# Attention times V with V as the stationary operand: four heads in 32-column tiles, output as head dimension by token

## The chip, the cores and the metric

The kernel runs on one core of a Trainium2 chip. The metric is the device time of one execution in microseconds (us), measured several times. Where a ratio of two kernels is given, it is the mean time of the fast runs of one over that of the fast runs of the kernel before in the same rounds, so it is not quite the ratio of the medians that are quoted beside it.

The engines are named as the profile names them: PE is TensorE (matmul), PEld its weight loads, DVE is VectorE, ACT is ScalarE, POOL is GpSimd, SP only issues DMAs.

## The reference

One transformer-like block over 2048 tokens of width 576: windowed attention with 32 heads of 18 elements, gated by a feed-forward network.

```python
def _A_ref(x, wqkv, wo):                      # x: layernormed, (1, 2048, 576)
    H = 32; Dh = 18; W = 256
    q, k, v = ...                             # x @ wqkv, split in heads
    scores = einsum("bhqd,bhkd->bhqk", q, k) * Dh ** -0.5
    mask = (0 <= i - j) & (i - j < W)
    p = softmax(where(mask, scores, -1e9))
    o = einsum("bhqk,bhkd->bhqd", p, v)
    return o.transpose(0, 2, 1, 3).reshape(B, S, D) @ wo
def _B_ref(x, w_gate, w_up, w_down):          # F = 4608
    return (sigmoid(x @ w_gate) * (x @ w_up)) @ w_down
out = x + _A_ref(xn, ...) * silu(_B_ref(xn, ...))
```

## The kernel before

The program is written as a graph of operations, each with an engine, an estimated duration and dependencies. A list scheduler in the kernel's own Python puts them in a fixed order on each engine, using the estimates; on the chip each engine then runs its list in order and waits on semaphores. Work goes in four blocks of 512 tokens. Attention goes by groups of four heads (8 groups per block, 32 in all), and the feed-forward matmuls (gate/up, then down) of the block stand between its pieces.

PSUM is cut into two pools of two units (a unit is two banks): pool S for attention, projections and transposes, pool F for the feed-forward network.

```python
self.pool_s = Pool("S", [0, 1])
self.pool_f = Pool("F", [2, 3])
```

A score visit computes up to four 128x128 blocks for four heads and takes **both** units of pool S:

```python
h = self.pool_s.hold(2)
...            # matmuls with 32-row tiles, then exp on ACT, mask multiply on DVE
```

The product with V (PV) uses the exponentials as the stationary operand, so the output has tokens on partitions. The last column of V is ones, which gives the softmax sum beside each output. Three small VectorE operations normalise; the unit of PSUM is free after the first of them.

```python
hp = self.pool_s.hold()
def f_pv(eng):                                 # 96 matmuls with 19 columns per group (72 in the first block)
    for i in range(BPC):
        for h4 in range(4):
            for n, kb in enumerate(kbs):
                res = pair(eng, [b[:, o:o + 19] for b in outs],
                           lambda r, t: self.expr[r, se, h4, at * P:(at + 1) * P],
                           lambda r, t: self.v_aug[r, kb % NVB, hg * 4 + h4, :], ...)
sm = op("DVE", dve_ns(608), f_sum, ...)        # adds the two row halves, PSUM -> SBUF
hp.release(sm)
rc = op("DVE", 120, lambda e: e.reciprocal(self.rrec[:, sr, :], out[:, :, DH]), ...)   # 128x16
on = op("DVE", dve_ns(288), f_on, ...)         # o_tok = pvs * rrec
```

After the eight groups, each 128 tokens are transposed on PE (18 small matmuls), copied out of PSUM by VectorE and multiplied with wo.

The softmax here doesn't subtract the row's maximum and nothing guards it: scores larger than these inputs give would overflow.

## Time and profile before

The median is 602.46 us (three runs, 599.55 to 611.99, the last of them slow). The profiled execution took 602.5 us, of which 600.8 us are in the trace.

| | before |
|---|---|
| span of the trace | 600.8 us |
| PE / DVE / ACT / POOL busy | 98% / 55% / 50% / 26% |
| chain of waits that ended last | 94% PE |
| mean granted PE clock | 0.992 |

The busy line of the page, and below it the waits view for PE (engine and line, what it waited for, us in total, number of times, longest):

```profile
PE 587.5 (98%) x10424; PEld 345.8 (58%) x10424; DVE 329.5 (55%) x631; ACT 297.8 (50%) x397; POOL 156.9 (26%) x316
```

```profile
PE ps L62 <- DMA wgs<-in_B_w_up_dram: 3.5, 2, 2.4
PE ps L434 <- DVE xnr L405: 1.7, 2, 0.9
...
```

PE is the limit, and it waits for almost nothing: about 8 us in all. What PV costs is read from the timeline of PE (start us, length us, engine, line, operation, tiles, count). One head group, in the second block:

```profile
214.68 1.36 PE L62 MATMUL ps<-v_aug,expr 64*128 64x19 bf16 x96
215.89 2.10 PE L62 MATMUL ps<-xnT,wgs 64*128 64x512 bf16 x18
217.93 0.40 PE L565 MATMUL ps<-qT,kT 18*128 18x256 bf16 x12
218.26 2.98 PE L62 MATMUL ps<-xnT,wgs 64*128 64x512 bf16 x26
```

Lengths overlap by the depth of the pipeline, so starts are what to subtract: PV holds PE from 214.68 to 215.89, which is 1.21 us; a score visit holds it for 0.33 us. The VectorE part of the same work, from the groups of instructions (busy us, mean ns of one, idle before):

```profile
L620 DVE TENSOR_REDUCE pvs<-ps 128x304 f32<-128x608 f32 x32 | 25.3, 791 | 16.2 <-PE ps L62 16.2
L632 DVE TENSOR_TENSOR o_tok<-pvs,rrec 128x288 bf16<-128x288 f32 x32 | 14.6, 458 | 1.1
L625 DVE RECIPROCAL rrec<-pvs 128x16 f32<-128x16 f32 x32 | 8.1, 254 | 1.1
```

### The profile page before, as it was taken

The page shows a single profiled execution, that of the slowest core. Times are in us where ns is not written, and L with a number is a line of the kernel's source. Part 1 is how long each engine was busy: PE and PEld are TensorE (multiplying, and loading weights), DVE is VectorE, ACT ScalarE, POOL GpSimd, SP SyncE. Part 2 cuts the span into 40 slices and gives each one's busy share as a digit, 9 for nine tenths or more (in the row PEclk, how much of TensorE's full clock was granted, in tenths as well). Part 3 has the DMA queues.
Part 4 walks back from the last instruction along what each step waited for, and adds up shares of the span by engine and source line. Part 5 has one row for each costly group of instructions (what it writes and reads, how often), then busy time and mean ns, then how long its engine had stood idle before and what let it go on. Part 6 is the DMA issues. An engine that isn't in the chain of part 4 may idle for free.

```text
span 600.8 us, 22967 instructions
## 1 busy us (share of the span) xinstructions
PE 587.5 (98%) x10424; PEld 345.8 (58%) x10424; DVE 329.5 (55%) x631; ACT 297.8 (50%) x397; POOL 156.9 (26%) x316
## 2 busy tenths in 40 slices
PE   6999999999999999999999999999999999999996
PEld 5554544577764444567775454446777545445775
DVE  4336576626567676554546666565444766556122
ACT  3135456455275666564265666564245565675111
POOL 3190410710554105200554005200555016000000
PEclk8999999999999999999999999999999999999999
DMA  9999999900044754540202565553020364650010
GB/s 192 191 199 214 212 208 220 175 8 23 24 119 118 184 131 113 135 102 2 61 20 60 138 142 129 134 123 82 21 58 25 96 143 105 158 122 4 2 42 21
DMA packets 112050, 63.89 MB, mean 106 GB/s; under 512 B 12208, under 2 KB 109936, under 8 KB 111952
## 3 DMA queue, kind: packets, MB, share of 16 engines
q1 hardware_dynamic: 101552, 57.08, 43.8%
q0 software_dynamic: 9216, 4.75, 3.4%
q8 instruction: 82, 1.34, 1.0%
q10 hardware_dynamic: 1184, 0.59, 0.5%
q14 instruction: 16, 0.13, 0.1%
HBM read 55.30 MB, written 2.36 MB: 96 GB/s over the span
## 4 chain that ended last, share of the span: by engine, by line
PE 94%; DMA 3%; DVE 1%; ACT 1%; issue 0%; SPq 0%; ACTq 0%; DVEq 0%
PE ps L62 87%; PE ps L565 5%; DMA wgs<-in_B_w_up_dram 3%; PE ps L434 1%; ACT expr L581 0%; SPq L206 0%; DVE pvs L620 0%; ACT L362 0%; DVE o_tok L632 0%; DVE s_attn L817 0%; DVE thf L822 0%; ACTq L206 0%; DVE hT L735 0%; ACT tring L732 0%; DVE rrec L625 0%
## 5 line engine op out<-in xcount | busy, mean ns | idle before, releaser
L62 PE MATMUL ps<-xnT,wgs 64*128 64x512 bf16 (+1 forms) x2628 | 300.3, 377 | 4.2 <-DMA wgs<-in_B_w_up_dram 3.5
L581 ACT ACTIVATE expr<-ps 128x1024 bf16<-128x1024 f32 (+1 forms) x192 | 179.5, 969 | 69.2 <-PE ps L565 69.2
L62 PEld LDWEIGHTS ps<-xnT,wgs 64*128 64x128 bf16 x2628 | 122.3, 95 | 144.4 <-issue 9.1
L62 PE MATMUL ps<-wd_sb,hT 64*128 64x288 bf16 x2304 | 151.9, 283 | 0.0
L589 DVE TENSOR_TENSOR expr<-expr,mask 128x768 bf16<-128x768 bf16 (+2 forms) x192 | 93.9, 491 | 103.4 <-ACT expr L581 103.2
L732 ACT ACTIVATE tring<-ps 128x512 bf16<-128x512 f32 x144 | 86.0, 597 | 124.4 <-PE ps L62 124.4
L206 POOL DMA_DIRECT2D qT<-qd x144 | 73.4, 509 | 280.0 <-DVE qd L471 156.5
L735 DVE SCALAR_TENSOR_TENSOR hT<-tring,ps 128x512 bf16<-128x512 bf16 x144 | 99.1, 688 | 58.8 <-ACT tring L732 56.2
L62 PEld LDWEIGHTS ps<-wd_sb,hT 64*128 64x128 bf16 x2304 | 108.3, 94 | 30.9 <-issue 3.5
L206 POOL DMA_DIRECT2D kT<-qd x144 | 73.3, 509 | 0.0
L62 PEld LDWEIGHTS ps<-v_aug,expr 64*128 64x128 bf16 x2880 | 41.0, 93 | 7.1 <-issue 1.2
L62 PE MATMUL ps<-v_aug,expr 64*128 64x19 bf16 x2880 | 41.3, 168 | 0.6 <-issue 0.6
L62 PE MATMUL ps<-xnT,wqk 64*128 64x512 bf16 (+1 forms) x360 | 38.1, 355 | 0.5 <-ACT expr L581 0.5
L565 PE MATMUL ps<-qT,kT 18*128 18x256 bf16 (+1 forms) x960 | 37.0, 245 | 0.0
L565 PEld LDWEIGHTS ps<-qT,kT 18*128 18x128 bf16 x960 | 15.7, 92 | 35.6 <-issue 21.9
L471 DVE CAST qd<-ps 128x1024 bf16<-128x1024 f32 (+1 forms) x20 | 22.3, 1117 | 24.9 <-PE ps L62 24.9
L620 DVE TENSOR_REDUCE pvs<-ps 128x304 f32<-128x608 f32 x32 | 25.3, 791 | 16.2 <-PE ps L62 16.2
L807 ACT ACTIVATE thf<-ps 128x576 bf16<-128x576 f32 (+1 forms) x20 | 11.1, 555 | 46.4 <-PE ps L62 45.9
L398 POOL TENSOR_TENSOR rstd<-veps,neghalf 128x1 f32<-128x1 f32 x16 | 9.0, 570 | 72.7 <-DVE veps L396 72.6
L673 ACT ACTIVATE s_attn<-ps 128x576 bf16<-128x576 f32 x16 | 10.4, 650 | 34.9 <-PE ps L62 34.9
L62 PEld LDWEIGHTS ps<-xnT,wqk 64*128 64x128 bf16 x360 | 17.2, 94 | 17.1 <-ACT expr L581 1.9
L420 ACT ACTIVATE xnT<-ps 128x1152 bf16<-128x1152 bf16 x15 | 16.4, 1130 | 8.5 <-PE ps L434 8.4
(45 smaller groups left out, 215.8 us busy)
## 6 DMA issues: line engine op xcount, KB each, us to landing
wgs<-in_B_w_gate_dram SPq DMA_DIRECT2D x71, 288.0 KB, 4.0
wgs<-in_B_w_up_dram SPq DMA_DIRECT2D x71, 288.0 KB, 4.8
wd_sb<-in_B_w_down_dram SPq DMA_DIRECT2D x9, 576.0 KB, 9.9
xf<-in_A_x_dram SPq DMA_DIRECT2D x16, 144.0 KB, 3.4
out_dram<-xf SPq DMA_DIRECT2D x16, 144.0 KB, 1.9
qT<-qd POOLq DMA_DIRECT2D x112, 18.0 KB, 2.0
kT<-qd POOLq DMA_DIRECT2D x112, 18.0 KB, 2.0
xr<-in_A_x_dram SPq DMA_DIRECT2D x6, 288.0 KB, 4.5
```

The costliest lines, as they stand in the source:

```text
L62: res = eng.matmul(outs[i], lhs(ROWS[t], i), rhs(ROWS[t], i), start=start, stop=stop, tile_position=(64 * t, 0))
L206: o = self.op(eng, DMA_ISSUE_NS[eng], lambda e: e.dma_start(dst, src), name, deps, prio, nbytes=nbytes)
L420: return eng.activation(dst, self.tr_src(h), ACTF.Copy)
L471: return eng.tensor_copy(dst, self.both(h, n))
L565: res = eng.matmul(self.ps[:, o:o + nq * P], self.kT[r, kp, ko:ko + P], self.qT[r, qs, q0 * P:(q0 + nq) * P], start=True, stop=True, tile_ ...
L581: return eng.activation(self.expr[:, se, 2 * u:2 * u + 2, 0:n], src, ACTF.Exp, scale=SM_SCALE)
L589: return eng.tensor_tensor(e_, e_, m_, ALU.mult)
L620: return eng.tensor_reduce(self.pvs[:, pt, :], self.both(hp, 304).rearrange("p t q -> p q t"), mybir.AxisListType.X, ALU.add)
L673: return eng.activation(dst, self.both(h2, 288), ACTF.Copy, scale=0.25)
L732: th = op("ACT", act_ns(NT), lambda e: e.activation(self.tring[:, st, :], bank(h, 0), ACTF.Tanh, scale=0.5), f"th:{c}:{ft}", deps=[pg, dt_ ...
L735: mu = op("DVE", dve_ns(NT), lambda e: e.scalar_tensor_tensor(self.hT[:, ft, :], self.tring[:, st, :], 1.0, bank(h, 1), ALU.add, ALU.mult) ...
L807: return e.activation(v2(t)[:, a:b, :], y2()[:, a:b, :], ACTF.Tanh, scale=0.25)
```

## The change

The intent is to take work off PE. V becomes the stationary operand: 19 columns, one 32-column tile per head, so that four heads run side by side, and the tokens stream. The output has the head dimension on partitions (32 per head) and the token along the free axis, which is what wo wants, so the transposes go. A shuffle spreads each head's sum over its 32 partitions, a reciprocal and a multiply normalise, and small DMAs pack the heads from 32-partition to 18-partition spacing. Bundled with it is a new start of the program: more warm-up matmuls used as fillers, three early gate/up tiles instead of two, and the first weights loaded from another queue. The scheduler's estimate for issuing a DMA on the GpSimd queue also goes from 1000 to 600 ns.

```diff
 hp = self.pool_s.hold()
 def f_pv(eng):
-    ... pair(eng, outs, expr (stationary), v_aug (19 moving columns)) ...
+    b = hp.units[0] * 1024
+    for n, (kb, q0, nq, se, at) in enumerate(blocks):
+        for h4 in range(4):
+            res = eng.matmul(self.ps[32 * h4:32 * h4 + DH + 1, b + q0 * P:b + (q0 + nq) * P],
+                             self.v_aug[:, kb % NVB, hg * 4 + h4, :], self.expr[:, se, h4, at * P:(at + nq) * P],
+                             start=(n == 0), stop=(n == len(blocks) - 1), tile_position=(0, 32 * h4), ...)
-sm = op("DVE", dve_ns(608), f_sum, ...)
-hp.release(sm)
-rc = op("DVE", 120, lambda e: e.reciprocal(self.rrec[:, sr, :], out[:, :, DH]), ...)
-on = op("DVE", dve_ns(288), f_on, ...)
+sh = op("DVE", 740, lambda e: e.stream_shuffle(self.den[:, :], pv_out(), [DH] * 32), ..., deps=[pv])
+rc = op("DVE", dve_ns(NT), lambda e: e.reciprocal(self.den[:, :], self.den[:, :]), ..., deps=[sh])
+on = op("DVE", dve_ns(NT), lambda e: e.tensor_tensor(self.onr[:, so, :], pv_out(), self.den[:, :], ALU.mult), ...)
+hp.release(on)
+... 160 DMAs on the GpSimd queue pack onr into oT ...
 def build_wo(self, c):
-    ... 16 x (18 transposes on PE, copy on DVE) ...
 # start of the program
-NWARM = 70
+NWARM = 110
-early = 2 if c == 0 else 0
+early = 3 if c == 0 else 0
 ... (cut)
```

`dve_ns(512)` is 673 ns. The unit of PSUM is now held until the last of the three VectorE operations, because the multiply reads PSUM.

More of the change, by code (lines that the diff above doesn't have):

```diff
@@ L37 @@
 NFIN = 2
-NWARM = 70
+NON = 2
+KT = 5
+COL = 1032
+NWARM = 110
 NQK = 5
-DMA_ISSUE_NS = {"SP": 600.0, "POOL": 1000.0, "ACT": 650.0}
+DMA_ISSUE_NS = {"SP": 600.0, "POOL": 600.0, "ACT": 650.0}
 DMA_LAT_NS = 2500.0
@@ L119 @@
     __slots__ = ("eng", "est", "deps", "fn", "name", "prio", "start", "end", "tok", "needs_tok",
-                 "nbytes", "slack", "idx", "succs", "cidx", "odeps", "acq", "lane", "mode")
+                 "nbytes", "slack", "idx", "succs", "cidx", "odeps", "acq", "lane", "mode", "filler")
     def __init__(self, eng, est, fn, name, deps, prio, nbytes, odeps, acq):
@@ L152, in __init__ @@
         self.slack = 0.0
+        self.filler = None
         for d in self.odeps:
@@ L238, in alloc_memory @@
         assert size([P, BPC, D], bf16) <= size([P, NEX, 4, NT], bf16)
-        self.o_tok, _ = seq("o_tok", [P, BPC, XW])
-        self.oT, _ = seq("oT", [P, 2, KS, P])
+        self.oT, _ = seq("oT", [P, KT, NT])
+        self.onr, _ = seq("onr", [P, NON, NT])
+        self.den, _ = seq("den", [P, NT], f32)
         self.s_attn, _ = seq("s_attn", [P, BPC, D])
@@ L243, in alloc_memory @@
         self.wv_sb, _ = seq("wv_sb", [P, KS, D // 2])
-        self.wo_sb, _ = seq("wo_sb", [P, KS, D // 2])
+        self.wo_sb, _ = seq("wo_sb", [P, KT, D])
         self.qd, _ = seq("qd", [P, NQD, 2, NT])
@@ L256, in alloc_memory @@
         self.rstd, _ = seq("rstd", [P, NST, 1], f32)
-        self.pvs, _ = seq("pvs", [P, 1, 4 * BPC * (DH + 1)], f32)
-        self.rrec, _ = seq("rrec", [P, 2, 4 * BPC], f32)
         if self.verbose:
@@ L272, in build_graph @@
         self.r_ex = Ring(NEX, "expr")
-        self.r_rec = Ring(2, "rrec")
-        self.r_pvs = Ring(1, "pvs")
-        self.r_oT = Ring(2, "oT")
+        self.r_on = Ring(NON, "onr")
         self.r_w = Ring(NWS, "wgs")
@@ L289, in build_graph @@
         self.op_q2 = {}
-        self.otr_last = []
+        self.wo_last = []
+        self.op_oT = []
         self.prev_f2_last = None
@@ L364, in build_consts @@
         h = self.pool_f.hold()
+        w = None
         for i in range(NWARM):
@@ L367, in f_warm @@
                 return pair(eng, self.halves(h, P), lambda r, t: zero[r, :], lambda r, t: zero[r, :], True, True)
-            w = op("PE", 110, f_warm, f"warm:{i}", deps=[z], prio=1, acq=None if i else h, odeps=[w] if i else [])
-        h.release(w)
-        self.ffn_last = w
+            w = op("PE", 110 if i < 36 else 64, f_warm, f"warm:{i}", deps=[z], prio=4, acq=None if i else h, odeps=[w])
+            w.filler = h
+            h.release(w)
         wq, wk, wv = (self.wqkv[:, i * D:(i + 1) * D] for i in range(3))
@@ L413, in f_tr @@
                 return self.transposes(eng, h, lambda r, o: self.xnr[r, sn, o:o + P])
-            tr = op("PE", KS * 29.5, f_tr, f"tr:{st}", deps=[dup, self.op_ident, war], prio=pr, acq=h)
+            tr = op("PE", KS * 29.5, f_tr, f"tr:{st}", deps=[dup, self.op_ident, war], prio=pr if c else 0, acq=h)
             self.r_xn.release(sn, tr)
@@ L551, in build_attn @@
             masks = [(0, 1, 2), (1, 3, 1), (0, 3, 1)]
-        where = {}
+        blocks = []
         ready = []
@@ L573, in build_attn @@
             se, de = self.r_ex.produce()
-            for at_, (kb, q0, nq, at) in enumerate(specs):
-                for i in range(nq):
-                    where[(kb, q0 + i)] = (se, at + i)
+            blocks += [(kb, q0, nq, se, at) for kb, q0, nq, at in specs]
             for u in range(2):
@@ L599, in f_pv @@
             res = None
-            outs = self.halves(hp, 304)
-            for i in range(BPC):
-                kbs = [kb for kb in (k0 + i - 2, k0 + i - 1, k0 + i) if kb >= 0]
+            b = hp.units[0] * 1024
+            for n, (kb, q0, nq, se, at) in enumerate(blocks):
                 for h4 in range(4):
-                    o = i * 76 + h4 * 19
-                    for n, kb in enumerate(kbs):
-                        se, at = where[(kb, i)]
-                        res = pair(eng, [b[:, o:o + 19] for b in outs],
-                                   lambda r, t: self.expr[r, se, h4, at * P:(at + 1) * P],
-                                   lambda r, t: self.v_aug[r, kb % NVB, hg * 4 + h4, :], n == 0, n == len(kbs) - 1)
-            return res
-        pv = op("PE", (48 if c else 36) * 24.7, f_pv, f"pv:{c}:{hg}", deps=[[m for m, _ in ready], vdeps], prio=1, acq=hp)
+                    res = eng.matmul(self.ps[32 * h4:32 * h4 + DH + 1, b + q0 * P:b + (q0 + nq) * P],
+                                     self.v_aug[:, kb % NVB, hg * 4 + h4, :], self.expr[:, se, h4, at * P:(at + nq) * P],
+                                     start=(n == 0), stop=(n == len(blocks) - 1), tile_position=(0, 32 * h4),
+                                     skip_group_check=True)
+            return res
+        pv = op("PE", 30 + sum(57 * b[2] for b in blocks), f_pv, f"pv:{c}:{hg}", deps=[[m for m, _ in ready], vdeps], prio=1, acq=hp)
+        pv.mode = COL
         self.op_pv[(c, hg)] = pv
@@ L614, in build_attn @@
             self.r_ex.release(se, pv)
-        sr, dr = self.r_rec.produce()
-        pt, dp = self.r_pvs.produce()
-        def f_sum(eng):
-            return eng.tensor_reduce(self.pvs[:, pt, :], self.both(hp, 304).rearrange("p t q -> p q t"),
-                                     mybir.AxisListType.X, ALU.add)
-        sm = op("DVE", dve_ns(608), f_sum, f"ps:{c}:{hg}", deps=[pv, dp], prio=1)
-        hp.release(sm)
-        out = self.pvs[:, pt, :].rearrange("p (q d) -> p q d", d=DH + 1)
-        rc = op("DVE", 120, lambda e: e.reciprocal(self.rrec[:, sr, :], out[:, :, DH]), f"rc:{c}:{hg}",
-                deps=[sm, dr], prio=1)
@@ L628, in f_on @@
-        def f_on(eng):
-            src = out[:, :, 0:DH].rearrange("p (q h) d -> p q h d", q=BPC)
-            dst = self.o_tok[:, :, hg * 72:(hg + 1) * 72].rearrange("p q (h d) -> p q h d", d=DH)
-            rr = self.rrec[:, sr, :].rearrange("p (q h) -> p q h", q=BPC)[:, :, :, None].broadcast_to([P, BPC, 4, DH])
-            return eng.tensor_tensor(dst, src, rr, ALU.mult)
-        on = op("DVE", dve_ns(288), f_on, f"on:{c}:{hg}", deps=[rc, self.otr_last], prio=1)
-        self.r_rec.release(sr, on)
@@ L635, in build_attn, with pv_out @@
-        self.r_pvs.release(pt, on)
-        self.op_on[(c, hg)] = on
+        so, do = self.r_on.produce()
+        def pv_out():
+            b = hp.units[0] * 1024
+            return self.ps[:, b:b + NT]
+        sh = op("DVE", 740, lambda e: e.stream_shuffle(self.den[:, :], pv_out(), [DH] * 32), f"den:{c}:{hg}", deps=[pv], prio=1)
+        rc = op("DVE", dve_ns(NT), lambda e: e.reciprocal(self.den[:, :], self.den[:, :]), f"rc:{c}:{hg}", deps=[sh], prio=1)
+        on = op("DVE", dve_ns(NT), lambda e: e.tensor_tensor(self.onr[:, so, :], pv_out(), self.den[:, :], ALU.mult),
+                f"on:{c}:{hg}", deps=[rc, do], prio=1)
@@ new lines, in build_attn @@
+        hp.release(on)
+        for u in range(4 * hg, 4 * hg + 4):
+            d0, end = DH * u, DH * u + DH
+            while d0 < end:
+                d1 = min(end, (d0 // P + 1) * P)
+                p0 = 32 * (u % 4) + d0 - DH * u
+                for r0 in ((d0 % P,) if d0 < 4 * P else (d0 % P, 64 + d0 % P)):
+                    o = self.dma(self.oT[r0:r0 + d1 - d0, d0 // P, :], self.onr[p0:p0 + d1 - d0, so, :], (d1 - d0) * NT * 2,
+                                 f"dma:o:{c}:{u}", ("o", hg), deps=[on, self.wo_last], prio=1, eng="POOL")
+                    self.r_on.release(so, o)
+                    self.op_oT.append(o)
+                d0 = d1
@@ L637, in build_attn @@
         if (c, hg) == (0, 0):
-            self.op_wo_w = self.load_rows(self.wo_sb, self.wo[:, 0:288], self.wo[:, 288:D], "dma:wo", ("wo",), 8, [pv])
+            self.op_wo_w = [self.dma(self.wo_sb[:, 0:4, :], self.wo[0:512, :].rearrange("(k p) c -> p k c", p=P), 512 * D * 2,
+                                     "dma:wo", ("wo", 0), deps=[pv], prio=8)]
+            self.op_wo_w += [self.dma(self.wo_sb[r, 4, :], self.wo[512:D, :], 64 * D * 2, "dma:wo4", ("wo", 1), deps=[pv],
+                                      prio=8) for r in ROWS]
@@ L640, in build_wo @@
     def build_wo(self, c):
         op = self.op
-        last = []
-        dup = op("DVE", 280, lambda e: e.tensor_copy(self.o_tok[:, :, D:XW], self.o_tok[:, :, 0:64]), f"odup:{c}",
-                 deps=[self.op_on[(c, 0)], self.otr_last], prio=1)
-        for i in range(BPC):
-            qb = c * BPC + i
-            h = self.pool_s.hold()
-            so, do = self.r_oT.produce()
-            def f_tr(eng, i=i, h=h):
-                return self.transposes(eng, h, lambda r, o: self.o_tok[r, i, o:o + P])
-            tr = op("PE", KS * 29.5, f_tr, f"otr:{qb}", deps=[[self.op_on[(c, hg)] for hg in range(NHG)], dup, self.op_ident],
-                    prio=1, acq=h)
-            last.append(tr)
-            def f_te(eng, h=h, so=so):
-                dst = self.oT[:, so, :, :].rearrange("p k (t c) -> p t k c", t=2)
-                return eng.tensor_copy(dst, self.tr_src(h))
-            te = op("DVE", dve_ns(KS * P, 1.9), f_te, f"ote:{qb}", deps=[tr, do], prio=1)
-            h.release(te)
-            h2 = self.pool_s.hold()
-            ss = i
-            war = [self.op_q2[qb - BPC]] if c else []
-            def f_wo(eng, h2=h2, so=so):
-                return self.row_proj(eng, h2, lambda r, kt: self.oT[r, so, kt, :], self.wo_sb)
-            wo = op("PE", 9 * mm_ns(288), f_wo, f"wo:{qb}", deps=[te, self.op_wo_w, war], prio=1, acq=h2)
-            self.r_oT.release(so, wo)
-            def f_se(eng, ss=ss, h2=h2):
-                dst = self.s_attn[:, ss, :].rearrange("p (t c) -> p t c", t=2)
-                return eng.activation(dst, self.both(h2, 288), ACTF.Copy, scale=0.25)
-            se = op("ACT", act_ns(D), f_se, f"sev:{qb}", deps=[wo], prio=1)
-            h2.release(se)
-            self.op_s[qb] = se
@@ L677, in build_wo, with wo, f @@
-        self.otr_last = last
+        oT, self.op_oT, self.wo_last = self.op_oT, [], []
+        def wo(i, h, swap, deps, acq):
+            cols = slice(i * P, (i + 1) * P)
+            ks = range(KT - swap)
+            def f(eng):
+                res = None
+                for k in ks:
+                    res = pair(eng, self.halves(h, 288), lambda r, t: self.oT[r, k, cols],
+                               lambda r, t: self.wo_sb[r, k, 288 * t:288 * t + 288], swap == 0 and k == 0,
+                               swap == 1 and k == KT - 2, swap)
+                return res
+            return op("PE", len(ks) * mm_ns(288), f, f"wo:{c * BPC + i}:{swap}", deps=[oT, self.op_wo_w, deps], prio=1, acq=acq)
@@ new lines, in build_wo, with f_se @@
+        for i in range(0, BPC, 2):
+            hs = [self.pool_s.hold() for _ in range(2)]
+            lo = [wo(i + j, hs[j], 0, [self.op_q2[c * BPC + i + j - BPC]] if c else [], hs[j]) for j in range(2)]
+            for j in range(2):
+                qb = c * BPC + i + j
+                hi = wo(i + j, hs[j], 1, [lo[j]], None)
+                self.wo_last.append(hi)
+                def f_se(eng, i=i, j=j, h=hs[j]):
+                    dst = self.s_attn[:, i + j, :].rearrange("p (t c) -> p t c", t=2)
+                    return eng.activation(dst, self.both(h, 288), ACTF.Copy, scale=0.25)
+                se = op("ACT", act_ns(D), f_se, f"sev:{qb}", deps=[hi], prio=1)
+                hs[j].release(se)
+                self.op_s[qb] = se
@@ L687, in build_ffn, with pe @@
             self.op_wd = []
-        def pe(est, fn, name, deps, acq=None):
-            o = op("PE", est, fn, name, deps=deps, prio=3, odeps=[self.ffn_last], acq=acq)
+        def pe(est, fn, name, deps, acq=None, prio=3):
+            o = op("PE", est, fn, name, deps=deps, prio=prio, odeps=[self.ffn_last], acq=acq)
             self.ffn_last = o
@@ L695, in weights @@
             sw, dw = self.r_w.produce()
-            pr = wg if c == 0 and wg < 4 else 3
+            pr = 1 + wg if c == 0 and wg < 4 else 3
             fc = slice(wg * WG * P, (wg + 1) * WG * P)
-            ds = self.load_rows(self.wgs[:, sw, :, :], self.wg[:, fc], self.wu[:, fc], f"dma:w:{c}:{wg}", ("w", sw), pr,
-                                [dw, self.op_tab if c == 0 and wg == 0 else None],
-                                eng="ACT" if c == 0 and wg == 0 else "SP")
+            ds = self.load_rows(self.wgs[:, sw, :, :], self.wg[:, fc], self.wu[:, fc], f"dma:w:{c}:{wg}", ("w", sw), pr, [dw])
             slots[wg] = sw
@@ L727, in f @@
                 return res
-            return pe(len(ks) * mm_ns(n), f, f"f1{half}:{c}:{ft}", [xin, wops[ft // WG]], acq)
+            return pe(len(ks) * mm_ns(n), f, f"f1{half}:{c}:{ft}", [xin, wops[ft // WG]], acq,
+                      3 if part is None else 1)
         def tail(ft, h, pg):
@@ L740, in tail @@
             hm[ft] = mu
-        early = 2 if c == 0 else 0
+        early = 3 if c == 0 else 0
         if early:
             weights(0)
-            hs = [self.pool_f.hold() for _ in range(early)]
+            weights(1)
+            hs = [self.pool_f.hold() for _ in range(2)] + [self.pool_s.hold()]
             for part in range(2):
@@ L751, in build_ffn @@
                         tail(ft, hs[ft], u)
-            self.r_w.release(slots[0], u)
+                    if part and ft == 1:
+                        self.r_w.release(slots[0], u)
         for ft in range(early, NFT):
-            if ft % WG == 0:
+            if ft % WG == 0 and ft // WG not in slots:
                 weights(ft // WG)
@@ L880, in schedule @@
                 mode = o.mode
+                if o.name.startswith("f1"):
+                    for d in [d for d in ops if d.filler is not None and d.idx < 0]:
+                        d.filler.rel.remove(d)
+                        d.idx = nsched
+                        nsched += 1
+                        if d in enabled["PE"]:
+                            enabled["PE"].remove(d)
             enabled[o.eng].remove(o)
@@ L904, in schedule @@
             for e in ENGS:
-                busy = sum(o.est for o in prog[e])
+                busy = sum(o.est for o in prog[e] if o.filler is None)
                 print(f"[sched] {e}: n={len(prog[e])} busy={busy / 1e3:.1f}us end={max(o.end for o in prog[e]) / 1e3:.1f}us")
```

## The prediction

> **What bounds it now.** TensorE. The page gives PE 98% busy over a 600.8 us span, and the chain of waits is 94% PE; the waits view finds only about 8 us of PE waiting (3.5 us of it on weight DMAs). VectorE is 55% busy, ScalarE 50%, GpSimd 26%. So a PE microsecond is worth a microsecond, unless another engine comes onto the chain.
>
> **What the change takes off PE.**
> - PV: in the timeline, 96 matmuls of 19 columns hold PE 1.21 us per head group (0.90 us, 72 matmuls, in the first block): 36 us in all. As four concurrent column tiles, 12 blocks of 128 tokens should stream like the score matmuls, whose 4-block visits take 0.33 us including a mode change of about 0.11 us each way (estimate from the timeline: 0.213 us of streaming). So PV costs about 0.64 + 0.22 + some issue = 0.9 us (0.7 in the first block). Saving about 0.3 x 24 + 0.18 x 8 = 9 us, although it adds 62 mode changes (192 to 254 in the PE order).
> - The 16 output transposes, 0.25 us each: 4 us.
> Sum: about -13 us, 589 us alone.
>
> **What it adds to VectorE.** Per head group it drops the reduce (0.79), small reciprocal (0.25) and normalise (0.46), plus 0.75 us per transpose eviction; it adds a shuffle of 512 (about 0.7), a 512 multiply (0.69, as the 512-wide products now) and a reciprocal of 128x512. The reciprocal decides. Today a 128x16 one takes 254 ns, always, while a 128x1 VectorE operation takes 148 ns and other operations fit 150 ns plus one cycle per element. The excess is 106/15 = 7 ns per element. The Trainium skill ("VectorE: DVE Perf Modes", the 8-slice pipeline) says reciprocal is an iterative divide with a repeat count of 8; the trace agrees in size. Estimate: 145 + 511 x 7.1 = 3.8 us (8 cycles: 4.4 us).
>
> **Why that lands on the critical path.** The PV PSUM unit is held until the multiply ends, about 0.2 + 0.7 + 3.8 + 0.7 = 5.5 us after PV. Score visits need both units of that pool, and the PE order puts the next one after 26 to 28 gate/up matmuls (2.9 to 3.1 us) or 40 down matmuls (2.45 us). PE, in order, stalls 2.5 to 3 us per head group; going through the order by group, with some in the first block and the last group shielded, I get about 80 us (97 at 4.4 us). Gate/up tiles waiting for VectorE's product are hit inside the same stall. VectorE goes to about 430 us busy. The packing DMAs (2.0 us to landing now) should cost little.
>
> Prediction: 602 - 13 + 80 + about 5 for backlog = 675 us, range 635 to 705. Faster by over 2%: 0.12; within 2%: 0.05; slower by over 2%: 0.83. If reciprocal streams one element per cycle, about 589 us.
>
> **What would show it.** Groups: reciprocal 128x512 mean 3.5 to 4.4 us, 32 of them (0.7 refutes me); shuffle about 0.7 us; PV about 0.9 us from its start to the next matmul in the timeline. Waits: PE at the score matmuls waiting on the VectorE multiply into onr, some 30 times, 2 to 4 us each, about 80 us in total. Chain: VectorE reciprocal with over 15%.
>
> **What would make it wrong.** Reciprocal pipelined at full rate (the excess 106 ns being fixed); column tiles not running concurrently (PV then 2.5 us, another 40 us); PE clock dropping in the repeated stalls; head-of-line blocking in the GpSimd queue.

## The result, and the profile after

The changed kernel takes 690.84 us (median of four runs, 690.1 to 695.67), before 603.21 us in the same comparison; the ratio is 1.149, with a 95% interval of 1.141 to 1.158. Executions over 1.5% slower than the fastest of the same kernel are left out of the means. The record has no check of its output; honest_est below, which runs the same operations in another order, is correct.

The busy line after:

```profile
PE 603.3 (88%) x8238; PEld 336.1 (49%) x8238; DVE 418.6 (61%) x643; ACT 300.1 (44%) x397; POOL 238.2 (35%) x476
```

No engine is near its limit any more: PE fell from 98% to 88% of a longer span, and VectorE is at 61%. This fits a chain in which engines wait for each other; the timeline has to show it. PE is also busy for longer than before with fewer instructions. The new VectorE groups:

```profile
L619 DVE RECIPROCAL den<-den 128x512 f32<-128x512 f32 x32 | 107.3, 3353 | 1.1
L620 DVE TENSOR_TENSOR onr<-ps,den 128x512 bf16<-128x512 f32 x32 | 22.1, 690 | 1.1
L618 DVE STREAM_SHUFFLE den<-ps 128x512 f32<-128x512 f32 x32 | 23.3, 727 | 0.0
```

The reciprocal takes 3.353 us, five times what the scheduler believed. One head group in the timeline, PE and VectorE; the bracket at the end of a line gives the idle time before the instruction and what ended it:

```profile
306.19 0.84 PE L603 MATMUL ps<-expr,v_aug 128*19 128x256 bf16 x32
306.96 2.63 PE L65 MATMUL ps<-wd_sb,hT 64*128 64x288 bf16 x40
...
307.09 0.73 DVE L618 STREAM_SHUFFLE den<-ps 128x512 f32<-128x512 f32 x1
307.85 3.35 DVE L619 RECIPROCAL den<-den 128x512 f32<-128x512 f32 x1
311.23 0.69 DVE L620 TENSOR_TENSOR onr<-ps,den 128x512 bf16<-128x512 f32 x1
...
312.07 0.40 PE L568 MATMUL ps<-qT,kT 18*128 18x256 bf16 x12 [2.49 <-DVE onr L620]
...
312.40 4.29 PE L65 MATMUL ps<-wd_sb,hT 64*128 64x288 bf16 x40
...
316.96 2.62 PE L65 MATMUL ps<-wd_sb,hT 64*128 64x288 bf16 x40
```

PV itself became faster, as intended: it holds PE from 306.19 to 306.96, 0.77 us instead of 1.21. Then PE runs 40 down matmuls and arrives at the score visit, which needs both units of pool S. One of them is held until the multiply ends at 311.92, so PE is idle for 2.49 us. And then something more: the 40 down matmuls after the stall take 4.29 us, the same 40 a little later 2.62 us. The windows view of those stretches (window, its length, PE busy and instructions, the same for the other engines, then the granted PE clock) shows why:

```profile
309.60:312.00 2.40, 0.00 (x0) 0.00 (x0) 2.29 (x2) 0.00 (x0) 0.00 (x0) 1.00 0.00 0
312.45:313.50 1.05, 1.05 (x17) 0.77 (x16) 0.00 (x0) 0.98 (x2) 1.05 (x3) 0.76 0.13 31
313.50:314.50 1.00, 1.00 (x12) 0.64 (x10) 0.57 (x2) 0.96 (x2) 0.72 (x2) 0.50 0.16 37
314.50:315.50 1.00, 1.00 (x12) 0.66 (x10) 0.55 (x1) 0.00 (x0) 0.00 (x0) 0.50 0.09 21
```

After the stall PE runs at half its clock. Before the end of the program the clock record of this trace has 18 such half-clock stretches of 3.41 us each, and their starts lie whole multiples of 3.41 us apart. Cut the trace on that grid, and the idle time can be set beside each fall; here are the fall above and a later one, each below the stretch in front of it (windows view, columns as before):

```profile
309.59:313.00 3.41, 0.93 (x22) 0.76 (x24) 2.30 (x2) 0.48 (x1) 0.78 (x2) 1.00 0.00 0
313.00:316.41 3.41, 3.41 (x34) 2.17 (x29) 1.12 (x2) 1.46 (x2) 1.22 (x3) 0.50 0.11 27
364.21:367.62 3.41, 1.04 (x24) 0.60 (x22) 3.02 (x3) 0.12 (x1) 1.19 (x3) 1.00 0.06 15
367.62:371.03 3.41, 3.41 (x26) 1.70 (x22) 1.54 (x3) 2.46 (x3) 3.41 (x8) 0.50 0.27 76
```

PE idles for 2.48 and 2.37 us of the stretches in front. In this trace a fall followed each stretch of the grid with 2.04 us of idle time or more, and only one of the 13 with 1.5 to 2.0 us. So not each long stall brings a fall: the longest, 3.62 us from 75.56 to 79.17, lies across two stretches (1.93 and 1.69 us), and the clock stays at 1.00. This is no exact limit: in free_psum and warm_stall some falls follow stretches with 1.1 to 1.9 us. The mean clock of the whole run is 0.955, before it was 0.992. In the waits view of PE, the stalls on the multiply lead by far:

```profile
PE ps L568 <- DVE onr L620: 56.7, 25, 3.6
PE ps L437 <- DVE onr L620: 4.7, 3, 2.3
PE ps L65 <- DVE hT L727: 2.7, 4, 2.1
...
```

### The profile page after: what moved, and what is told of

It is laid out like the page before. It is cut to its first block, busy times and chain, and to the rows that moved or that the text cites. A ratio compares the mean times of both kernels' runs of the same rounds, so it can differ in the third digit from the quotient of the medians.

```text
span 689.0 us, 18796 instructions
## 1 busy us (share of the span) xinstructions
PE 603.3 (88%) x8238; PEld 336.1 (49%) x8238; DVE 418.6 (61%) x643; ACT 300.1 (44%) x397; POOL 238.2 (35%) x476
## 3 DMA queue, kind: packets, MB, share of 16 engines
q8 instruction: 65, 1.06, 0.7%
HBM read 55.37 MB, written 2.36 MB: 84 GB/s over the span
## 4 chain that ended last, share of the span: by engine, by line
PE 65%; DVE 25%; DMA 3%; issue 3%; POOL 2%; SPq 2%; ACT 1%; DVEq 0%
PE ps L65 58%; DVE den L619 15%; PE ps L568 4%; DVE den L618 3%; DVE onr L620 2%; DVE qd L474 2%; PE ps L603 2%; SPq L210 2%; DMA wqk<-in_A_wqkv_dram 2%; DVE hT L727 1%; DMA kT<-qd 1%; ACT tring L724 1%; ACT expr L581 1%; POOL qT L210 1%; POOL oT L210 1%
## 5 line engine op out<-in xcount | busy, mean ns | idle before, releaser
L65 PE MATMUL ps<-xnT,wgs 64*128 64x512 bf16 (+1 forms) x2646 | 317.2, 390 | 4.7 <-DVE hT L727 2.7
L65 PEld LDWEIGHTS ps<-xnT,wgs 64*128 64x128 bf16 x2646 | 128.1, 98 | 160.3 <-issue 34.5
L210 POOL DMA_DIRECT2D oT<-onr x160 | 80.6, 511 | 294.6 <-DVE onr L620 263.2
L65 PE MATMUL ps<-wd_sb,hT 64*128 64x288 bf16 x2304 | 159.4, 292 | 0.0
L65 PEld LDWEIGHTS ps<-wd_sb,hT 64*128 64x128 bf16 x2304 | 115.8, 97 | 32.8 <-issue 4.2
L619 DVE RECIPROCAL den<-den 128x512 f32<-128x512 f32 x32 | 107.3, 3353 | 1.1
L603 PE MATMUL ps<-expr,v_aug 128*19 128x256 bf16 (+1 forms) x960 | 25.5, 247 | 0.0
L618 DVE STREAM_SHUFFLE den<-ps 128x512 f32<-128x512 f32 x32 | 23.3, 727 | 0.0
```

The costliest lines, as they stand in the source:

```text
L65: res = eng.matmul(outs[i], lhs(ROWS[t], i), rhs(ROWS[t], i), start=start, stop=stop, tile_position=(64 * t, 0))
L210: o = self.op(eng, DMA_ISSUE_NS[eng], lambda e: e.dma_start(dst, src), name, deps, prio, nbytes=nbytes)
L603: res = eng.matmul(self.ps[32 * h4:32 * h4 + DH + 1, b + q0 * P:b + (q0 + nq) * P], self.v_aug[:, kb % NVB, hg * 4 + h4, :], self.expr[:, ...
L618: sh = op("DVE", 740, lambda e: e.stream_shuffle(self.den[:, :], pv_out(), [DH] * 32), f"den:{c}:{hg}", deps=[pv], prio=1)
L619: rc = op("DVE", dve_ns(NT), lambda e: e.reciprocal(self.den[:, :], self.den[:, :]), f"rc:{c}:{hg}", deps=[sh], prio=1)
```

## The experiments

Theory A: the long reciprocal keeps the PV unit of PSUM taken, PE stalls at the next score visit, and its clock falls after stalls. Theory B: something else in the change costs the time (the 62 additional changes of the tiling mode, the column tiles themselves, the 160 packing DMAs, the new start). Inside theory A there are rivals too: is it the held PSUM, the one long VectorE instruction that others queue behind, or only the wrong estimate in the scheduler?

All runs were compared with the kernel before on the same chip; the medians of before in the three sets were 602.26, 605.62 and 601.66 us. The kernels called wrong give a wrong result; the other experiments are correct.

| kernel | PSUM unit held to | reciprocal | scheduler believes | median us | ratio to before | clock |
|---|---|---|---|---|---|---|
| the change | multiply | 512 | 673 ns | 690.84 | 1.149 | 0.955 |
| cheap_inv (wrong) | multiply | none, a maximum | 673 ns | 590.5 | 0.980 | 0.997 |
| half_inv (wrong) | multiply | 256 of 512 | 673 ns | 612.24 | 1.017 | 0.991 |
| warm_stall | multiply | 512 | 673 ns | 670.76 | 1.113 | 0.981 |
| honest_est | multiply | 512 | 3353 ns | 679.04 | 1.126 | 0.952 |
| free_psum | copy | 512 | 673 ns | 655.35 | 1.081 | 0.963 |
| free_honest | copy | 512 | 3353 ns | 615.08 | 1.021 | 0.994 |
| free_split | copy | 4 x 128 | 4 x 954 ns | 593.64 | 0.981 | 0.998 |
| split_held | multiply | 4 x 128 | 4 x 954 ns | 697.87 | 1.158 | 0.929 |
| block_t | first transpose | 16 | 254 ns | 591.33 | 0.977 | 0.994 |
| before_start | (before) | (before) | (before) | 603.89 | 0.999 | 1.000 |

### cheap_inv: everything but the reciprocal

```diff
-e.reciprocal(self.den[:, :], self.den[:, :])
+e.tensor_tensor(self.den[:, :], self.den[:, :], self.den[:, :], ALU.max)      # wrong on purpose
```

> The 128x512 reciprocal is replaced by a 128x512 maximum of the tile with itself ([...]the result is wrong on purpose); the order of instructions on every engine is the same. Theory A (the reciprocal holds the PV unit of PSUM, PE stalls at the next score visit, its clock then falls): the replaced operation takes 0.69 us, the multiply ends about 2.4 us after PV, PE waits for it under 5 us in all (56.7 now), the clock is back at 0.99, and the time is 588 us (580 to 597). Theory B (column tiles, 62 more mode changes, 160 packing DMAs or the new start cost it): over 650 us.

Measured: 590.5 us, ratio 0.980 (0.974 to 0.987). PE's waits for the multiply are 1.0 us in all. The line of the waits view, and the busy line:

```profile
PE ps L568 <- DVE onr L620: 1.0, 1, 1.0
PE 571.7 (97%) x8238; PEld 323.5 (55%) x8238; DVE 335.2 (57%) x643; ACT 298.0 (51%) x397; POOL 237.9 (40%) x476
```

Theory B is out: with the column tiles, the mode changes, the packing DMAs and the new start all in place, the kernel is 2% faster than before. The one operation that differs costs 100 us. Since this kernel runs the same instructions in the same order as the change, apart from that one operation, the two busy lines split those 100 us: the spans are 689.0 and 588.5 us, a difference of 100.5; PE's idle time is 689.0 - 603.3 = 85.7 against 588.5 - 571.7 = 16.8, so 68.9 us are idle time; the other 31.6 us are the same matmuls running longer (the profile models where a matmul ends, so the split is not exact). The clock record accounts for most of the 31.6: in the change PE is busy for 61.0 us inside the half-clock stretches, here for 3.4 us, so by estimate the half clock costs 30.5 and 1.7 us, a difference of 28.8.

### half_inv: half the dose

```diff
-e.reciprocal(self.den[:, :], self.den[:, :])
+e.reciprocal(self.den[:, 0:256], self.den[:, 0:256])                          # wrong on purpose
```

> The reciprocal of only the first 256 of 512 columns (wrong result on purpose), same order on every engine. The reciprocal takes 0.154 + 256 x 6/960 = 1.75 us. Theory A with a threshold: the multiply ends about 3.4 us after PV, where PE arrives at the score visit 2.5 to 3.1 us after PV, so the stall is 0.4 to 0.9 us per group, 15 us in all, too short for the clock to fall: 603 us (595 to 615). If the loss is linear in VectorE time: 588 + (1.75 - 0.69)/(3.35 - 0.69) x 102 = 629 us.

Measured: 612.24 us; the reciprocal took 1.753 us, as computed, and PE waited 16.8 us for the multiply at score visits:

```profile
PE ps L568 <- DVE onr L620: 16.8, 25, 2.0
```

The time lies between the two expectations, but the curve is bent as the threshold demands: the first 1.06 us of added VectorE time (0.69 to 1.75) cost 21.7 us, or 20 us per microsecond; the next 1.60 us (1.75 to 3.35) cost 78.6 us, or 49 per microsecond. There are only 32 head groups, so pure waiting could not cost more than 32 per microsecond. The rest must come from something that long stalls bring with them; before its end this trace has three half-clock stretches, where the change has 18.

### warm_stall: fill the stalls

34 dummy matmuls stand in front of each wait of a score visit for the multiply. They write the second bank of the PV unit, which nothing uses, so the order of everything else is the same.

```diff
+ds = [d for d in o.deps if d.name.startswith("on:")]          # in front of the waits of a score visit
+...
+for _ in range(NDUM):                                         # 34
+    eng.matmul(self.ps[:, b:b + P], self.ident[ROWS[0], :], self.ident[ROWS[0], :], start=True, stop=True, ...)
```

> 34 dummy matmuls of 128 columns (about 1.9 us) stand on PE in front of each wait of a score visit for the multiply (27 places), writing the unused bank of the PV unit; everything else is the same, in the same order. If part of the loss is the clock that falls after each stall (mean 0.955 here, 0.992 before, 26 us of PE time by that difference): the clock is back at 0.98 or more, PE's waits shrink by what the dummies fill, VectorE's chain is the same, and the time falls to 665 us (655 to 678). If the clock has nothing to do with the stalls, or the whole loss is waiting: 690 us or a little more.

Measured: 670.76 us, 20 us less than the change with more work on PE, and the mean clock rose from 0.955 to 0.981. In the group that was shown above the dummies run from 307.69, the wait shrinks to 0.60 us, and the 40 down matmuls that follow take full speed:

```profile
307.69 2.06 PE L921 MATMUL ps<-ident 64*128 64x128 bf16 x34
310.34 0.40 PE L569 MATMUL ps<-qT,kT 18*128 18x256 bf16 x12 [0.60 <-DVE onr L621]
310.68 2.62 PE L66 MATMUL ps<-wd_sb,hT 64*128 64x288 bf16 x40
```

So the loss has two parts, and the second is real: stalls of about two microseconds often bring PE a lower clock afterwards. The half-clock time before the end falls from 61.4 to 23.9 us, in five stretches, four of which follow stalls at other operations, where no dummies stand. By the estimate used above, the half clock now costs 11.6 us instead of 30.5, which is about the 20 us that were gained.

### honest_est: only the estimate corrected

```diff
-rc = op("DVE", dve_ns(NT), lambda e: e.reciprocal(...), ...)
+rc = op("DVE", 3353, lambda e: e.reciprocal(...), ...)
```

> Only the scheduler's estimate of the reciprocal is corrected, from 673 to 3353 ns; the operations are the same, their order on the engines is not. If the loss is a matter of order (the list scheduler put the next score visit 2.5 to 3.1 us behind PV because it took the reciprocal for short): the stalls go from 57 us to under 15 us and the time to 615 us (600 to 640), with PSUM still held 5 us. If VectorE cannot do the work in time whatever the order: over 660 us.

Measured: 679.04 us. My 615 us was wrong, and the other expectation had the right time but not the reason: VectorE is 61% busy, not full. The scheduler did move work between PV and the next score visit; from 172 to 335 us PE is busy for 153.7 us instead of 145.1, and the waits for the multiply fall to 5.2 us in all. But 22.5 us of waits of feed-forward matmuls for hT, VectorE's gate/up product, have come up, which the change had for 2.7 us. And with pool S taken for 5 us per group, attention lasts longer than the feed-forward work that can stand between its pieces, and at the end of the last block there is nothing left to put there. The last groups run bare, at half clock from 614.6 to 652.2 us, and wo then waits for the packing DMAs:

```profile
621.11 1.46 PE L603 MATMUL ps<-expr,v_aug 128*19 128x256 bf16 x32 [2.13 <-ACT expr L581]
627.61 0.61 PE L568 MATMUL ps<-qT,kT 18*128 18x256 bf16 x8 [5.04 <-DVE onr L620]
...
646.38 7.41 PE L65 MATMUL ps<-wo_sb,oT 64*128 64x288 bf16 x72 [11.40 <-DMA oT<-onr]
```

The order alone is not the cause; with PSUM held, a better order moves the stalls.

### free_psum: let go of PSUM, keep the rest

ScalarE copies the PV output to SBUF behind the shuffle, and the unit is free then, 1.5 us after PV in the group at 385 us (1.7 were expected). The reciprocal and its estimate stay.

```diff
+ev = op("ACT", act_ns(NT), lambda e: e.activation(ou[:, sv, :], pv_out(), ACTF.Copy), ..., deps=[sh, dv])
+hp.release(ev)
-on = ... e.tensor_tensor(self.onr[:, so, :], pv_out(), self.den[:, :], ALU.mult) ...
+on = ... e.tensor_tensor(self.onr[:, so, :], ou[:, sv, :], self.den[:, :], ALU.mult) ...
-hp.release(on)
```

> After the shuffle has read the sums, ScalarE copies the PV output to SBUF (bf16) and the PSUM unit is released there, about 1.7 us after PV; the multiply reads the copy. The reciprocal stays whole, 3.35 us on VectorE, and the scheduler still takes it for 0.67 us. If the held PSUM unit is the whole mechanism: PE hardly waits and the time is 592 us (586 to 600). If the occupied VectorE matters by itself (the gate/up products and masks queue behind the reciprocal and hold the other PSUM pool): the waits of the score visits for onr vanish, waits of the gate/up matmuls for hT of about 2 us in some 20 groups come up in their place, and the time is 625 us (605 to 650).

Measured: 655.35 us, 35 us better, a little above the range of the second expectation. That one named no loss of clock; the clock here is 0.963. The waits for the multiply are gone, and the ones that were named have taken their place:

```profile
PE ps L66 <- DVE hT L734: 29.5, 15, 2.7
PE ps L571 <- DVE qd L477: 11.0, 6, 2.2
...
```

The product of a gate/up tile, and the copy out of a q/k projection, now queue behind the reciprocal on VectorE, and hold their own PSUM. In the group at 385 us the reciprocal and its multiply occupy VectorE from 386.59 to about 390.6, the product starts at 390.59, and PE, idle for 2.30 us, goes on at 391.42. So held PSUM is not the whole mechanism: one long instruction on an in-order engine holds everything behind it.

### free_honest, free_split and split_held: the estimate, the pieces, the PSUM

These three, with the ones above, set the three suspects against each other. free_honest is free_psum with 3353 as estimate. free_split cuts the reciprocal in four of 128 columns and tells the scheduler; split_held does the same but holds PSUM until the multiply.

```diff
+rc = sh
+for i in range(4):
+    rc = op("DVE", 954, reciprocal of den[:, i * 128:(i + 1) * 128], ..., deps=[rc])
```

> As the kernel that frees PSUM early, and the reciprocal is cut into four of 128 columns (0.95 us each, 0.45 us more in all) with that estimate told to the scheduler, so that gate/up products run between them. If waits behind one long VectorE instruction are what is left when PSUM is free: 600 us (592 to 612), and clearly under the kernel with the whole reciprocal. If VectorE's total work is the limit: no better than that kernel.

> PSUM freed early as in the kernel of 655 us, the reciprocal whole (3.35 us), but its true length told to the scheduler. It tells apart what made the kernel with four pieces fast (594 us): the pieces, or the true estimate. If the pieces matter (a gate/up product that comes up during one long instruction waits up to 3.35 us whatever the order, and there are only two gate/up units in PSUM): 620 us (605 to 645), with waits of gate/up matmuls for hT left. If the estimate alone did it: 594 us (590 to 600).

> Four pieces of 128 columns with the true estimate, as in the kernel of 594 us, but the PV unit of PSUM is held until the multiply, as in the change. If holding PSUM costs time by itself even when nothing waits behind one long instruction: the score visits start 5 us or more after PV, attention stretches until the last head groups run without other work for PE as with the corrected estimate (679 us), and the time is 640 us (615 to 670). If the long instruction was all: 594 us (590 to 602).

Measured: 593.64, 615.08 and 697.87 us.

Where PSUM is free, the true estimate takes 655 to 615 us, and the pieces take 615 to 594. In free_honest 22.1 us of waits of gate/up matmuls for hT are left; in free_split none of note, although VectorE is busy for 412.0 us, as long as in free_psum (412.6). Cutting the reciprocal also changes the scheduler's order, so the 21 us are those of the pieces and of the order that they allow. VectorE had the time all along; it did not have it when it was asked.

Where PSUM is held, neither brings the time near that of before: 691, 679 and 698 us. I had expected 640 for split_held. Its trace shows the end of honest_est, longer: the last three groups run bare, with waits of about 2 us for exponentials and of 5.5 us for the multiply, and a clock of 0.75 from 600 us to the end.

```profile
625.01 1.46 PE L603 MATMUL ps<-expr,v_aug 128*19 128x256 bf16 x32
631.99 0.61 PE L568 MATMUL ps<-qT,kT 18*128 18x256 bf16 x12 [5.51 <-DVE onr L624]
634.74 0.62 PE L568 MATMUL ps<-qT,kT 18*128 18x256 bf16 x8 [2.14 <-ACT expr L581]
```

Its median is 19 us above that of honest_est, and PE's idle time accounts for most of it: 101.9 us against 82.7 in the profiled executions. The waits for hT are nearly gone (0.3 us against 22.5), as the pieces should do, but PE also runs bare at the ends of the second and third block (10.3 us of stalls each, at 318.7 to 330.8 and 479.3 to 491.4 us), where honest_est has 2.1 and 4.3 us, and for longer at the end. Why the scheduler leaves so little work for these ends is not settled; the chain is only 0.45 us longer per group, and the order differs throughout.

### block_t: a version without the long reciprocal

VectorE can transpose 32x32 blocks. Transposed so, the sum of each token stands in one column of its 32-token block, 16 per partition, and the reciprocal has 16 elements again. The result is multiplied in and transposed back; the PSUM unit is free after the first transpose.

```diff
-sh, rc, on as above
-hp.release(on)
+tin = op("DVE", dve_ns(NT), lambda e: e.transpose(ot[:, :], pv_out()), ...)
+hp.release(tin)
+ob = ot[:, :].rearrange("p (b j) -> p b j", j=32)
+rc = op("DVE", 254, lambda e: e.reciprocal(self.den[:, :], ob[:, :, DH]), ...)
+mu = op("DVE", dve_ns(NT), on_t = ob * self.den[:, :, None].broadcast_to([P, 16, 32]), ...)
+on = op("DVE", dve_ns(NT), lambda e: e.transpose(self.onr[:, so, :], self.on_t[:, :]), ...)
```

> A version meant to beat both: VectorE transposes the PV output in 32x32 blocks (PSUM to SBUF, then the unit is released), takes the reciprocal of the 16 sums per partition, multiplies with a broadcast, and transposes back; no 512-wide reciprocal. Both theories of the cause expect: transposes about 0.7 us each, reciprocal 0.25 us, the chain 2.4 us against 4.8 us, PSUM held 0.9 us after PV, PE waits as in the kernel with the cheap operation or less, clock 0.99, time 588 us (582 to 594), a correct result, VectorE busy about 341 us. If the block transposes are slow (over 2 us each): over 610 us.

Measured: 591.33 us (median of six runs, 589.65 to 594.64), correct; before in the same rounds 605.62 us; ratio 0.977, 95% interval 0.971 to 0.983. It is faster than both kernels; whether the gain over before reaches 2% is not decided, since the interval ends at 0.983. The groups:

```profile
L621 DVE STREAM_TRANSPOSE ot<-ps 128x512 f32<-128x512 f32 x32 | 22.8, 712 | 10.8 <-PE ps L605 10.8
L628 DVE STREAM_TRANSPOSE onr<-on_t 128x512 bf16<-128x512 bf16 x32 | 22.7, 708 | 0.6
L625 DVE TENSOR_TENSOR on_t<-ot,den 128x512 bf16<-128x512 f32 x32 | 22.1, 692 | 1.1
L624 DVE RECIPROCAL den<-ot 128x16 f32<-128x16 f32 x32 | 8.1, 253 | 1.1
```

The chain is 0.71 + 0.25 + 0.69 + 0.71 = 2.36 us instead of 4.77 us, VectorE is 339.3 us busy, and the waits view has no wait of PE for these tiles. free_split, at 0.981 of before, is not told apart from it by these runs.

### before_start: the new start alone

The kernel before with only the start of the change (fillers, three early tiles, weights from the other queue); the order of PE's first instructions is the one of the change; the estimate for GpSimd DMAs is left as it was.

> The kernel before with only the start-up part of the change (110 warm-up matmuls as fillers, three early gate/up tiles, weights on the SP queue), attention untouched. The trace of before has clock 0.60 and 0.72 at 10 to 20 us and PE busy 19.2 of the first 25 us; after the change clock 1.0 and 20.7 us. Expected: 599.5 us against 602.3 (-2 to -4 us); if the start is not on the critical path because the first block waits for weights later: no change.

Measured: 603.89 against 605.62 us, ratio 0.999 (0.994 to 1.003). If the start is worth 2 us, it is not told apart from nothing; it does not carry the gain of the other kernels.

## Why the prediction was right

The predicted time was 675 us with a range of 635 to 705; measured were 690.84. The mechanism was the one that the experiments confirm, but the sum was put together from terms of which two were off in opposite directions: 11 us too much for idle time, 27 us too little for what it called backlog. That 675 came within 16 us of the measured time is in part luck.

- **What PE saves: 13 us predicted.** cheap_inv, which has all of the savings and none of the loss, has a ratio of 0.980, about 12 us of 602. Right. PV was to cost 0.9 us with its mode changes; it holds PE for 0.77 us from its start, and the mode change in front of it takes about 0.1 us by estimate (28 gate/up matmuls take 3.13 us up to a score visit, 221.50 to 224.63 before, and 3.03 us up to the old PV, which needed no change, 211.65 to 214.68). The Trainium skill, "TensorEngine Tiling (Array Packing)", says under Key Properties that changing the tiling mode drains the engine; this case puts about 0.1 us on it.
- **The reciprocal: 3.8 us predicted, 3.353 measured.** It was read off one line of the profile before, 254 ns for 16 elements. With 16, 128, 256 and 512 columns it takes 254, 950, 1753 and 3353 ns: 6.25 ns per element, and 154 ns fixed. The estimate had taken too small a fixed part from other operations, so 7.1 ns per element came out.
- **PE's idle time: 80 us predicted, 68.9 measured** (from the busy lines of the change and cheap_inv). This is the first mis-sized term, and most of it is the previous one passed on: the chain is about half a microsecond shorter than assumed, in the 25 to 32 groups that wait for it. The place was right: 25 waits of score visits for the multiply into onr, up to 3.6 us, and a few more at transposes.
- **"Backlog": 5 us predicted; in its place 31.6 us of slower matmuls.** This is the second mis-sized term. The prediction named a dropping PE clock only under what would make it wrong. The Trainium skill, "TensorE: Matmul & The Clock Gate", gives in its table of the clock states that PE falls to half its clock after at least one idle window of about 3.4 us. The trace agrees on the half (0.50 in the windows shown) but not on how long PE must idle: stalls of 1.9 to 2.6 us came before all 18 falls, most of them whole within one stretch of the grid shown above, and one of 3.62 us across two stretches brought none. The measurement decides. warm_stall shows that the idle time is what brings it, and the half clock costs 28.8 of the 31.6 us by estimate.
- **VectorE busy: 430 us predicted, 418.6 measured**, and the reciprocal's share of the chain was to be over 15%: the page has 15%.
- **The packing DMAs were to cost little.** In cheap_inv they are all there, and PE's waits view has none for packed heads; in the change, with the long chain, it is 1.5 us.

What the prediction had not seen is how the two ways of the loss stand to each other. It wrote that the gate/up products "are hit inside the same stall", which is true as long as PSUM is held, and hides that they are a second cause: when PSUM was freed, they came up by themselves with 29.5 us of waits, and with 22.5 us in honest_est, where PSUM was still held but the order was better.

## What to carry to other kernels

Before a small operation is made wider, divide its measured time by its elements: a 254 ns reciprocal of 16 elements looked like nothing, and its 6.25 ns per element became 107 us of VectorE time when the layout gave it 512. Length on an engine that is not the bottleneck costs time in three ways that a busy share doesn't show: by the PSUM that is held until it ends, by what queues behind it in order, and by the clock that PE loses while it waits; so release PSUM first, cut long instructions where others must pass, and give the scheduler true durations. And when a layout change makes one part slow, change that part's layout back locally: two 0.71 us block transposes cost less than one 3.35 us reciprocal.

## What the Trainium skill lacked or had wrong

- "VectorE: DVE Perf Modes" says that reciprocal is an iterative divide with a repeat count of 8, but has no time for it. Measured in fp32 on 128 partitions: 254, 950, 1753 and 3353 ns for 16, 128, 256 and 512 columns, that is 154 ns + 6.25 ns per column, where a multiply of 512 columns takes 690 ns. Eight cycles at the 0.96 GHz that the page states would be 8.3 ns; the measured slope is 6 cycles.
- "TensorE: Matmul & The Clock Gate" warns of idle gaps over about 3 us and names an idle window of about 3.4 us. Here 2.04 us or more of idle time within one stretch of a 3.41 us grid brought PE to half its clock for 3.41 us each time, 18 times in all with one fall after 1.93 us, while a stall of 3.62 us across two stretches did not; by estimate this cost 28.8 us in 100 us of loss.
- The same page counts on dense work to keep the clock; filling a wait in mid-kernel with dummy matmuls is not in it. 34 dummy matmuls in front of each long wait brought the mean clock from 0.955 to 0.981 and the time from 690.8 to 670.8 us.
- "TensorEngine Tiling (Array Packing)" says that a mode change drains, without a figure: about 0.1 us, by estimate, in front of PV here. No page has a measured case of four 128x32 column tiles: PV with 12 blocks of 128 tokens for four heads took 0.77 us from its start to the next matmul.
- "VectorE: DVE Perf Modes" gives 311 ns for a 128x128 bf16 block transpose. For 128x512: 712 ns from PSUM in fp32, 708 ns in bf16.
